# A fixed four-engine order for the prologue of a fused attention and two-MoE kernel, with three weight slices of the first batch ahead of the rest, and two attention units scored a phase earlier

## The chip, the cores and the metric

The kernel runs on one core of one Trainium2 chip. The metric is the device time of one execution in microseconds (us); the time of a kernel is the median of its runs. A profile is one execution taken by the hardware profiler; its span runs from the first to the last instruction. Engines: PE (matmul), PEld (its weight loads), DVE, ACT, POOL, and SP, which issues all the DMAs.

## The reference

```python
def _attn_ref(q, k, v, phi):                  # 4 batches, 8 heads, 576 rows, head_dim 64, 32 memory slots
    a = np.exp(phi - phi.max(axis=2, keepdims=True))
    a = a / (a.sum(axis=2, keepdims=True) + 1e-09)
    k_m = np.einsum('bhsm,bhsd->bhmd', a, k)
    v_m = np.einsum('bhsm,bhsd->bhmd', a, v)
    scores = 1 / np.sqrt(64) * np.matmul(q, k_m.transpose(0, 1, 3, 2))
    attn = np.exp(scores - scores.max(axis=-1, keepdims=True))
    attn = attn / (attn.sum(axis=-1, keepdims=True) + 1e-09)
    return np.matmul(attn, v_m)
# its output as 2304 tokens x 512, then
h = np.maximum(np.maximum(x @ w1, x @ w2), x @ w3);  x = h @ w_out         # 512 -> 768 -> 512
h = x @ w_in;  y = (np.maximum(h, 0) + np.log1p(np.exp(-np.abs(h)))) @ w_out2   # 512 -> 2048 -> 512
```

## The kernel before

**Units.** The attention is cut into eight units: unit u is batch u // 2 and four of its heads. For each unit the code has these steps: `load_phi`, `load_x` (i = 0 is k, i = 1 is v) and `load_q` issue its DMAs; `att_max` and `att_exp` make exp(phi - max); `att_x` multiplies that with k or v (its first call also makes the column sums) and scales the result into `kvd`; `att_tr` turns it into `kT` or into a part of the tile `v`; `att_q` transposes q on PE and ACT copies it into `qT`; `att_sc` makes the scores; `att_sm0`, `att_sm1`, `att_sm2` are the softmax over the 32 slots (transposes and maximum on DVE; subtraction on POOL or DVE, then exp on ACT; sum and reciprocal on DVE, then the multiplication); `att_fin` transposes on DVE into `aT` and splits the result into a high part `ah` (ACT) and a rest `al`.

**First MoE, by pairs of batches.** `pp` 0 is units 0 to 3 (batches 0 and 1), `pp` 1 is units 4 to 7. attn @ v_m is never made. Instead, for each of six slices j of 128 columns of w1, w2 and w3, the slice is multiplied with v_m (`u_mm`, `u_mr`; L545 and L563 to L565) into a tile pair `uh`, `ul`, and `m1(i, bl, c)` multiplies that with `ah` and `al` (L591): 18 matmuls of 128x288, three products for each float32 product; then ACT and DVE take the maximum of the three results (L597 to L599) out of PSUM into `h`. Here i is 0 to 5 for `pp` 0 and 6 to 11 for `pp` 1, bl the batch of the pair (bl 0 reads units 0 and 1, bl 1 units 2 and 3), c the half of its rows. `phase_a` runs what is left of the 24 m1 of a pair, each a numbered slot; `phase_o` runs the 18 slots of `m1out` (L633 to L635), 12 matmuls of 128x384 each. So the program is: prologue, `phase_a(0)`, `phase_o(0)`, `phase_a(1)`, `phase_o(1)`, and then 96 equal blocks of the second MoE (L843, L875).

**Weights.** They come as 64-bit floats, as pairs of int32. `w_load(i, hf)` fetches half a slice with three DMAs into one of two buffers `wraw`; `w_conv` and `Conv.a` make floats of it: an ACT scaling of the upper word (L242), then two DVE operations (L245, L246), the last of which frees the buffer. A slice has four parts p of 128 rows.

**What sets the order.** A scheduler orders the instructions of each engine before the program runs, by its own estimate of when each can start and by the order in which the code writes them. For the prologue that order is the list `PLAN`, a row for each step (`ax` for `att_x`, `ca` for a conversion, and so on). In the phases the tables `C["att"]`, `C["scs"]`, `C["wo"]` give the slot behind which a step is written: `att` the first part of units 4 to 7, all in `phase_a(0)`; `scs` the six steps from `att_q` to `att_fin` of units 4 to 7, all in `phase_o(0)`; `wo` the conversions of w_out. On the chip each engine goes through its list in that order. PSUM gives PE six buffers for u, m1 and m1out (`psm`) and two (`pst`) for the rest from unit 4 on.

Of the kernel before, what the change touches and what calls it, by code (L numbers as in the profile page):

```python
# [20 lines left out]
PLAN = [  # L21
    ('ph', 0),
    ('ph', 1),
    ('wl', 0, 0),
    ('ld', 0, 1),
    ('ld', 1, 1),
    ('ph', 2),
    ('wl', 0, 1),
    ('ld', 0, 0),
    ('ld', 1, 0),  # L30
    ('q', 0),
    ('q', 1),
# [96 lines left out]
    'wo_off': {(4, 0): 1, (5, 3): 0, (5, 1): -1, (3, 3): -1, (3, 0): 0, (4, 1): -2, (3, 2): 0, (5, 0): -1, (3, 1): 1, (5, 2): -2, (4, 3): 0, (4, 2): 0},  # L129
# [6 lines left out]
def fused_kernel(ctx: ExitStack, tc: tile.TileContext, q, k, v, phi, w1, w2, w3, w_out, m_in, m_out, out):  # L136
# [82 lines left out]
    class Conv:  # L219
# [14 lines left out]
        def a(self):  # L234
            raw, n = self.raw, self.n
# [28 lines left out]
    @contextmanager  # L264
    def behind(u):
        with ExitStack() as st:
            for i in INS[u]:
                st.enter_context(tc.issue_after(i))
            yield
# [58 lines left out]
    def att_max(u):  # L328
# [6 lines left out]
        nc.vector.tensor_tensor(out=mx[0:SREM], in0=mx[0:SREM], in1=ph[0:SREM, :, R4], op=ALU.max)  # L335
        st = pst()
        nc.tensor.matmul(st[:, 0:P], mx.rearrange("p h m -> p (h m)"), ident, start=True, stop=True)
        mc = t_p.tile([P, 1], F32, tag="mc", name="mc", bufs=2)
        nc.vector.tensor_reduce(out=mc, in_=st[:, 0:P], op=ALU.max, axis=AX.X)
        md = t_p.tile([P, P], F32, tag="md", name="md", bufs=2)  # L340
        nc.vector.tensor_scalar(out=md, in0=ident, scalar1=mc, scalar2=None, op0=ALU.mult)
        nc.tensor.matmul(st[:, P:2 * P], onesq, md, start=True, stop=True)
        d["ma"] = st[:, P:2 * P].rearrange("p (h m) -> p h m", h=4)

    def att_exp(u):
        d = U[u]
        ph, ma = d.pop("ph"), d.pop("ma")
        nc.vector.tensor_tensor(out=ph, in0=ph, in1=ma.unsqueeze(2).to_broadcast([P, 4, R4 + 1, M]), op=ALU.subtract)
        et = t_p.tile([P, R4 + 1, 4, M], F32, tag="et", name="et", bufs=2)
        nc.scalar.activation(out=et.rearrange("p r h m -> p h r m"), in_=ph, func=AF.Exp)  # L350
        d["et"] = et.rearrange("p r h m -> p r (h m)")

    def att_x(u, i):
# [14 lines left out]
        if new_ri:  # L368
            for r in range(R4 + 1):
                for h in range(4):  # L370
                    a = slice(32 * h, 32 * h + 32)
                    k = slice(0, P if r < R4 else SREM)
                    nc.tensor.matmul(xp[a, D:D + 2], et[k, r, a], ones[k], start=(r == 0), stop=(r == R4))
            ri = t_p.tile([P, 1], F32, tag="ri", name="ri", bufs=2)
            nc.vector.tensor_scalar(out=ri, in0=xp[:, D:D + 1], scalar1=1e-9, scalar2=None, op0=ALU.add)
            nc.vector.reciprocal(out=ri, in_=ri)
            d["ri"] = ri
        kvd = t_p.tile([P, D], F32, tag="kvd", name="kvd", bufs=3)
# [3 lines left out]
    def att_tr(u, i):  # L382
# [5 lines left out]
        for s in range(2):  # L388
            nc.tensor.matmul(st[64 * s:64 * s + 64, P:2 * P], kvd, pick2[:, s], start=True, stop=True)
        sv = st[:, P:2 * P].rearrange("p (a c) -> p a c", a=2)  # L390
# [14 lines left out]

    def att_kv(u):
        att_x(u, 1)
        att_x(u, 0)

    def att_trs(u):  # L410
        att_tr(u, 1)
        att_tr(u, 0)

    def att_q(u, remeng="act"):
# [10 lines left out]
        for s in range(2):  # L425
            qp = ps()
            for r in range(R4):
                nc.tensor.transpose(qp[:, r * P:(r + 1) * P], x[:, s, r], ident)
            cast("act", qT[:, s, 0:R4 * P], qp)
        rem = ps()  # L430
        for s in range(2):
            nc.tensor.transpose(rem[:, s * SREM:(s + 1) * SREM], xr[:, 2 * s:2 * s + 2].rearrange("p h d -> p (h d)"), ident[0:SREM, 0:SREM])
        cast(remeng, qT[:, :, R4 * P:S], rem[:, 0:2 * SREM].rearrange("p (s c) -> p s c", s=2))
        d["qT"] = qT

    def att_sc(u):
# [4 lines left out]
        for c in range(2):  # L441
# [4 lines left out]
            d["sc"].append(sc)  # L446

    def att_sm0(u):
# [8 lines left out]
        d["mx"] = mx  # L457

    def att_sm1(u, sub="pool"):
# [3 lines left out]
        e.tensor_tensor(out=sT, in0=sT, in1=d.pop("mx").to_broadcast([P, NJB, 32]), op=ALU.subtract)  # L463
        nc.scalar.activation(out=sT, in_=sT, func=AF.Exp, scale=SCALE)

    def att_sm2(u, mul="pool"):
# [5 lines left out]
        nc.vector.reciprocal(out=sm, in_=sm)  # L472
        e = nc.vector if mul == "dve" else nc.gpsimd
        e.tensor_tensor(out=sT, in0=sT, in1=sm.to_broadcast([P, NJB, 32]), op=ALU.mult)

    def att_fin(u, lo="dve"):
# [74 lines left out]

    def u_mr(i, p):
# [23 lines left out]
    def m1(i, bl, c):  # L576
        pp, j = i // NJ, jof(i)
# [18 lines left out]
        h = h_t[j][:, o:o + HS]  # L596
        nc.scalar.activation(out=t0, in_=xs[0], func=AF.Copy)  # L597
        nc.vector.tensor_tensor(out=t0, in0=t0, in1=xs[1], op=ALU.max)
# [58 lines left out]
    def phase_a(pp, bg, us):  # L657
# [4 lines left out]
        def add_conv(slot, i, p):  # L662
            o = slot + C["wo_off"].get((i, p), 0)
            bg2[o].append(lambda: conv(i, p))
            if pp:
                bg2[o + 1].append(lambda: CK["w", i, p].b())
# [6 lines left out]
        for j in range(1 if pp == 0 else 0, NJ):  # L673
# [4 lines left out]
            if i == 1:  # L678
                four = [(0, 1, 0), (0, 1, 1), (1, 1, 0), (1, 1, 1)]
            for n, a in enumerate(four):  # L680
                main.append(lambda i=i, a=a, n=n, nxt=nxt: (m1(*a), u2(i + 1, n - us) if nxt and n in (us, us + 1) else None))
            if j + 2 < NJ:
# [18 lines left out]
    def conv(i, p):  # L701
        w_conv(i, p)
        u = 1 if i == 1 else 3 if 2 < i < NJ else None
        if u is None:
            CK["w", i, p].a()
            return
        with behind(u):
            CK["w", i, p].a()

    new_vT(0)  # L710
    STEPS = dict(ph=load_phi, ld=load_x, q=load_q, mx=att_max, ex=att_exp, ax=att_x, tr=att_tr, qT=att_q,
                 sc=att_sc, s0=att_sm0, s1=att_sm1, s2=att_sm2, fin=att_fin, wl=w_load, ca=conv,
                 un=u_new, u=u_mm, m1=m1)
    for st in PLAN:
        f = STEPS[st[0]]
        if isinstance(st[-1], dict):
            f(*st[1:-1], **st[-1])
        else:
            f(*st[1:])
# [9 lines left out]
    bg[3].append(lambda: (new_vT(1), load_u(4)))  # L729
# [7 lines left out]
    def held(f, u):  # L737
        with behind(3):
            f(u)

    wcv = {}
    for j in range(NJ):
        def wo_go(j=j):
            wcv[j] = wo_conv(j)
            with behind(3):
# [4 lines left out]
    phase_a(0, bg, C["us0"])  # L750
    bg = defaultdict(list)
    load_q(4)
    for n in range(4):
        u = 4 + n
        for sl, fn in zip(C["scs"][n], (lambda u=u: att_q(u), lambda u=u: (att_sc(u), load_q(u + 1) if u + 1 < 8 else None),
                                       lambda u=u: att_sm0(u), lambda u=u: att_sm1(u, C["s1"][u - 4]),
# [185 lines left out]
```

## Time and profile before

| | us |
|---|---|
| median of 3 runs | 743.45 (742.6 to 746.43) |
| profiled execution, whole | 743.82 |
| its span | 742.0 |
| PE busy | 705.8 |
| DVE, ACT, POOL busy | 406.4, 299.7, 250.0 |

What the profiled execution has beside its span is 1.82 us. A busy share over the whole span mixes stages with different limits, so the stages are read one by one: the prologue to about 56 us, `phase_a(0)` and what is left of the attention to 147.5, `phase_o(0)` to about 206, the passage into `phase_a(1)` to 236, its rest to 287.5, `phase_o(1)` to 340 and the second MoE to the end. The clock granted to PE has two levels in the records, 1.0 (2.4 GHz) and 0.5 (1.2 GHz); it is not recorded before 31.5 us. Transposes and other float32 matmuls of the attention have two records for each instruction, and a few records of m1 are missing.

### The profile page before, as it was taken

To read this page: it belongs to the slowest core of one execution; us is meant where nothing else is said; L and a number is where in the kernel's file an instruction comes from. 1 tells how busy PE (TensorE), PEld (TensorE's weight loads), DVE (VectorE), ACT (ScalarE), POOL (GpSimd) and SP (SyncE) were. 2 spreads that over 40 slices of the span, in tenths; PEclk is the share of its full clock that TensorE was granted. 3 is DMA by queue.
4 is the path that set the end of the run, shared out by engine and by line. 5 is a ranking of instruction groups with operands and counts; after the bars stand their busy time and mean duration, and the time that the engine had idled before them with its cause. 6 is when DMAs were issued, how large, how long until landed. Compare 5 with 4: busy or idle time off the path is not lost. (4 is left out here: it accounts for less than half of the span.)

```text
span 742.0 us, 12241 instructions
## 1 busy us (share of the span) xinstructions
PE 705.8 (95%) x4680; PEld 621.0 (84%) x4680; DVE 406.4 (55%) x780; ACT 299.7 (40%) x628; POOL 250.0 (34%) x239
## 2 busy tenths in 40 slices
PE   4879999999959999989999999999999999999997
PEld 3548777998848999978998988989888989898896
DVE  4557996425588974682333486333794334433343
ACT  2345555336458753552333453222442223222221
POOL 1112233035348414762222353222642223322221
PEclk9979999999988999999999999999999999999999
DMA  9998693502233200440000032000231000011112
GB/s 246 225 244 217 216 258 100 150 1 76 80 99 128 87 1 29 142 144 27 1 0 1 30 113 86 1 1 0 84 117 28 1 1 1 0 44 43 44 42 86
DMA packets 70490, 59.25 MB, mean 80 GB/s; under 512 B 27936, under 2 KB 65312, under 8 KB 70432
## 3 DMA queue, kind: packets, MB, share of 16 engines
q1 hardware_dynamic: 70432, 58.47, 27.3%
q8 instruction: 37, 0.61, 0.3%
q14 instruction: 21, 0.17, 0.1%
HBM read 53.74 MB, written 4.72 MB: 79 GB/s over the span
## 5 line engine op out<-in xcount | busy, mean ns | idle before, releaser
L217 POOL TENSOR_TENSOR gl<-m,gh 128x384 fp32r<-128x384 f32 x96 | 100.5, 1049 | 255.1 <-ACT gh L209 238.2
L849 DVE TENSOR_SCALAR e<-pst 128x384 int32<-128x384 int32 x96 | 53.1, 554 | 135.9 <-PE pst L843 135.8
L851 ACT ACTIVATE L<-e 128x384 f32<-128x384 f32 x96 | 50.3, 524 | 186.6 <-DVE e L849 186.5
L875 PE MATMUL acc<-oh,gh 128*128 128x512 f32 x288 | 113.7, 395 | 0.4 <-ACT gh L209 0.4
L875 PE MATMUL acc<-ol,gh 128*128 128x512 f32 x288 | 113.4, 394 | 0.0
L843 PE MATMUL pst<-yb,ih 128*128 128x384 f32 x384 | 102.1, 336 | 0.0
L591 PE MATMUL psm<-ah,uh 128*128 128x288 f32 x288 | 89.0, 314 | 9.7 <-ACT ah L485 6.9
L591 PE MATMUL psm<-al,uh 128*128 128x288 f32 x288 | 87.3, 304 | 0.6 <-POOL al L217 0.6
L591 PE MATMUL psm<-ah,ul 128*128 128x288 f32 x288 | 86.4, 302 | 0.0
L853 DVE SCALAR_TENSOR_TENSOR m<-pst,L 128x384 f32<-128x384 f32 x96 | 53.3, 556 | 56.0 <-ACT L L851 56.0
L875 PE MATMUL acc<-oh,gl 128*128 128x512 f32 x288 | 82.7, 394 | 0.0
L209 ACT ACTIVATE gh<-m 128x384 fp32r<-128x384 f32 x96 | 50.0, 523 | 63.1 <-DVE m L853 61.2
L843 PEld LDWEIGHTS pst<-yb,ih 128*128 128x128 f32 x384 | 70.0, 188 | 3.5 <-DVE m L853 0.7
L591 PEld LDWEIGHTS psm<-ah,uh 128*128 128x128 f32 x288 | 55.6, 195 | 17.0 <-ACT ah L485 7.7
L843 PE MATMUL pst<-y0h,ih 128*128 128x384 f32 x192 | 65.4, 341 | 2.6 <-DVE m L853 2.5
L843 PE MATMUL pst<-y0h,il 128*128 128x384 f32 x192 | 65.2, 340 | 0.0
L843 PE MATMUL pst<-y0l,ih 128*128 128x384 f32 x192 | 65.2, 340 | 0.0
L843 PE MATMUL pst<-yb,il 128*128 128x384 f32 x192 | 64.4, 335 | 0.0
L875 PEld LDWEIGHTS acc<-oh,gl 128*128 128x128 f32 x288 | 53.6, 187 | 11.4
L875 PEld LDWEIGHTS acc<-oh,gh 128*128 128x128 f32 x288 | 54.0, 187 | 10.5 <-ACT gh L209 0.9
L875 PEld LDWEIGHTS acc<-ol,gh 128*128 128x128 f32 x288 | 54.0, 187 | 9.0
L591 PEld LDWEIGHTS psm<-al,uh 128*128 128x128 f32 x288 | 56.1, 195 | 1.4 <-POOL al L217 1.0
(146 smaller groups left out, 1327.9 us busy)
## 6 DMA issues: line engine op xcount, KB each, us to landing
wraw<-in_moe_w_dram SPq DMA_DIRECT2D x66, 256.0 KB, 3.9
raw<-in_moe_w_in_dram SPq DMA_DIRECT2D x16, 512.0 KB, 3.7
raw<-in_moe_w_out_dram SPq DMA_DIRECT2D x16, 512.0 KB, 3.6
out_dram<-o SPq DMA_DIRECT2D x18, 256.0 KB, 2.2
kvm<-in_v_dram SPq DMA_DIRECT2D x8, 512.0 KB, 6.3
kvm<-in_k_dram SPq DMA_DIRECT2D x8, 512.0 KB, 7.1
wor<-in_moe_w_out_dram SPq DMA_DIRECT2D x6, 512.0 KB, 4.3
ph<-in_phi_dram SPq DMA_DIRECT2D x8, 256.0 KB, 5.8
```

What stands on the lines that cost most here:

```text
L209: nc.scalar.activation(out=dst, in_=src, func=AF.Copy)
L217: return e.tensor_tensor(out=dst, in0=src, in1=hi, op=ALU.subtract)
L591: nc.tensor.matmul(x, l[:, t, ws], r[:, cs], start=(n == 0), stop=(n == 5))
L843: nc.tensor.matmul(hx, l[:, ds], r[:, cs], start=(n == 0), stop=(n == 3 * ND - 1))
L849: nc.vector.tensor_scalar(out=e.bitcast(I32), in0=hx.bitcast(I32), scalar1=0x7FFFFFFF, scalar2=None, op0=ALU.bitwise_and)
L851: nc.scalar.activation(out=L, in_=e, func=AF.Softplus, scale=-1.0)
L853: nc.vector.scalar_tensor_tensor(out=m, in0=hx, scalar=0.0, in1=L, op0=ALU.max, op1=ALU.add)
L875: nc.tensor.matmul(acc[0][t], l[:, t * P:(t + 1) * P], r, **kw)
```

## The change

`PLAN` becomes a list of single-engine stages: each step is a generator that yields where it goes from one engine to the next, each repetition of a step in the list runs its next stage, and the whole list stands in a `manual_schedule` for PE, DVE, ACT and POOL, which keeps on these four the order in which the stages are written. SP is not among them. In the new list units 0 and 1 go first, with less in between; u(0) is made for bl 0 alone; then m1 of i = 0, 1 and 2 for bl 0; units 2 and 3 are finished among these; then bl 1. Fourteen slots stay for `phase_a(0)` instead of 20, and the tables are written anew for them. `scs` has negative numbers, which are slots of `phase_a(0)`: unit 4 is scored there except for its last step, unit 5 except for its last, unit 6 begins there; unit 7 keeps slots of `phase_o(0)`, but earlier ones.

```diff
 PLAN = [
-    ('ph', 0),
-    ('ph', 1),
-    ('wl', 0, 0),
...
+    ('ph', 0), ('ph', 1), ('ld', 0, 1), ('mx', 0), ('mx', 0), ('mx', 1), ('wl', 0, 0), ('mx', 0), ('mx', 1),
...
+    ('ca', 2, 1), ('m1', 1, 0, 0), ('sc', 3), ('wl', 3, 0), ('ax', 2, 0), ('ca', 2, 1), ('ax', 2, 0),
...
-    'load5': 5,
-    'att': [[9, 9, 10, 11, 11], [10, 12, 12, 13, 13], [13, 13, 15, 15, 15], [15, 18, 19, 21, 21]],
-    'wo': [[4, 5, 5], [6, 7, 7], [11, 11, 14], [11, 13, 17], [21, 22, 24], [23, 23, 23]],
-    'scs': [[4, 4, 4, 4, 5, 6], [5, 5, 5, 6, 6, 7], [6, 6, 6, 7, 10, 10], [8, 11, 12, 13, 14, 18]],
+    'load5': 0,
+    'cv0': {2: (0, 0, 1, 1), 3: (3, 4, 5, 6)},
+    'order': ('PE', 'DVE', 'Activation', 'Pool'),
+    'hold': (2, 3),
+    'att': [[1, 1, 2, 3, 3], [2, 4, 4, 5, 5], [6, 6, 8, 8, 8], [8, 10, 11, 12, 12]],
+    'wo': [[0, 1, 1], [2, 3, 3], [4, 5, 6], [6, 7, 8], [10, 11, 12], [12, 13, 13]],
+    'scs': [[-8, -7, -7, -6, -5, 0], [-6, -4, -4, -3, -2, 1], [-1, 0, 1, 2, 3, 4], [2, 4, 4, 5, 6, 8]],
+    'q4': 3,
...
+    def ca_step(i, hf):
+        cs = []
+        for p in (2 * hf, 2 * hf + 1):
+            cs.append(w_conv(i, p))
+            cs[-1].top()
+        yield
+        for c in cs:
+            c.join()
...
-    for st in PLAN:
-        f = STEPS[st[0]]
...
+    gens, DONE = {}, set()
+    order = {getattr(mybir.EngineType, x) for x in C["order"]}
+    with tc.manual_schedule(engines=order):
+        for st in PLAN:
+            if st[0] in LOADS:
+                LOADS[st[0]](*st[1:])
+                continue
+            if st not in gens:
+                gens[st] = STEPS[st[0]](*st[1:])
+            if next(gens[st], DONE) is DONE:
+                DONE.add(st)
...
-    bg[3].append(lambda: (new_vT(1), load_u(4)))
+    bg[0].append(lambda: (new_vT(1), load_u(4)))
...
+            (bg if sl < 0 else bgo)[sl + 14 if sl < 0 else sl].append(fn)
```

On SP, around the loads of the third weight slice (`wraw` is w1, w2, w3; `kvm`, `kvr` are k and v of a unit, `qn` and `qnr` q of units 0 to 3, `qr` of unit 4, `wor` the first part of w_out). Before:

```order
L183 DMA wraw<-in_moe_w_dram 128x2x256 x6
L183 DMA ph<-in_phi_dram 128x4x128
L183 DMA ph<-in_phi_dram 64x4x32
L183 DMA kvm<-in_v_dram 128x4x256
L183 DMA kvr<-in_v_dram 64x4x64
L183 DMA kvm<-in_k_dram 128x4x256
L183 DMA kvr<-in_k_dram 64x4x64
L183 DMA wor<-in_moe_w_out_dram 128x1024
```

Here the six `wraw` are the second slice; units 4 and 5, `wor` and q of unit 4 follow, and then the third slice, at the head of a row of twelve. The changed kernel, a few rows behind the second slice:

```order
L120 DMA ph<-in_phi_dram 128x4x128
L120 DMA ph<-in_phi_dram 64x4x32
L120 DMA kvm<-in_v_dram 128x4x256
L120 DMA kvr<-in_v_dram 64x4x64
L120 DMA kvm<-in_k_dram 128x4x256
L120 DMA kvr<-in_k_dram 64x4x64
L120 DMA wor<-in_moe_w_out_dram 128x1024
L120 DMA wraw<-in_moe_w_dram 128x2x256 x6
L120 DMA qr<-in_q_dram 128x4x64 x4
```

The first six rows are unit 5; unit 4 stands in the same form just ahead of them. So the third slice (the six `wraw`) still has units 4 and 5 and `wor` ahead of it; only q of unit 4 has gone behind it.

On ACT in the changed kernel, from the second m1 slice on. `wh` and `wl` from `wraw` are the conversion of the third slice, two instructions for each half; `mt` empties PSUM behind an m1, `kvd`, `kT`, `sT` and `v` are steps of units 2 and 3:

```order
L182 ACTIVATE wh<-wraw 128x384
L182 ACTIVATE wl<-wraw 128x384
L605 ACTIVATE mt<-psm 128x288
L182 ACTIVATE wh<-wraw 128x384
L182 ACTIVATE wl<-wraw 128x384
L330 ACTIVATE kvd<-psm,ri 128x64
L605 ACTIVATE mt<-psm 128x288
L345 ACTIVATE kT<-psm 128x128
L146 ACTIVATE hh<-h 128x384
L444 ACTIVATE sT<-sT 128x576
L330 ACTIVATE kvd<-psm,ri 128x64
L350 ACTIVATE v<-psm 128x2x64
```

Before, at its conversion of the third slice, ACT has the softmax of units 2 and 3 nearly behind it:

```order
L485 ACTIVATE ah<-aT 128x576
L464 ACTIVATE sT<-sT 128x576
L209 ACTIVATE hh<-h 128x384
L548 ACTIVATE uh<-psm 128x384 x3
L242 ACTIVATE wh<-wraw 128x384
L242 ACTIVATE wl<-wraw 128x384
L548 ACTIVATE uh<-psm 128x384
L242 ACTIVATE wh<-wraw 128x384
L242 ACTIVATE wl<-wraw 128x384
L597 ACTIVATE mt<-psm 128x288 x2
L485 ACTIVATE ah<-aT 128x576
```

The conversion of the third slice has moved ahead of the scores of units 2 and 3.

On PE at the passage from `phase_o(0)` to `phase_a(1)`, the scores of unit 7 (`pst<-qT,kT`). Before, they stand inside the m1 of the second pair:

```order
L565 MATMUL psm<-wl,vh 128x384
L444 MATMUL pst<-qT,kT 64x288 x2
L563 MATMUL psm<-wh,vh 128x384
L564 MATMUL psm<-wh,vl 128x384
L565 MATMUL psm<-wl,vh 128x384
L444 MATMUL pst<-qT,kT 64x288 x2
L591 MATMUL psm<-ah,uh 128x288 x2
```

In the changed kernel they stand among the matmuls of `m1out`, and some 40 further matmuls of `m1out` follow before the first m1:

```order
L643 MATMUL psm<-hh,wol_1526 128x384
L421 MATMUL pst<-qT,kT 64x288 x2
L644 MATMUL psm<-hlo,woh_1525 128x384
L642 MATMUL psm<-hh,woh_1525 128x384
L643 MATMUL psm<-hh,wol_1526 128x384
L644 MATMUL psm<-hlo,woh_1525 128x384
L642 MATMUL psm<-hh,woh_1525 128x384
L643 MATMUL psm<-hh,wol_1526 128x384
L421 MATMUL pst<-qT,kT 64x288 x2
L644 MATMUL psm<-hlo,woh_1525 128x384
```

Then come two m1 of bl 0 (36 matmuls) and 12 of L567 to L569, and only then the first m1 that reads units 6 and 7.

## Rows read from the trace of the kernel before

**Rows 1.** The profile's page: busy time of each engine, share of the span, instructions

```profile
PE 705.8 (95%) x4680; PEld 621.0 (84%) x4680; DVE 406.4 (55%) x780; ACT 299.7 (40%) x628; POOL 250.0 (34%) x239
```

**Rows 2.** Busy us by stretch (instructions), then granted clock, DMA share, GB/s

```profile
0.00:56.00 56.00, 39.73 (x599) 25.47 (x599) 28.29 (x76) 19.90 (x46) 6.95 (x17) 0.90 0.94 239
...
80.00:147.50 67.50, 67.22 (x762) 54.28 (x759) 50.87 (x130) 34.95 (x89) 18.55 (x23) 1.00 0.61 178
147.50:206.00 58.50, 58.34 (x462) 51.95 (x462) 25.05 (x50) 28.66 (x63) 25.48 (x24) 1.00 0.22 56
206.00:236.00 30.00, 20.96 (x113) 17.64 (x112) 24.98 (x44) 19.94 (x44) 17.30 (x17) 0.77 0.34 106
```

**Rows 3.** PE in order of time, 205 to 226 us [idle before, releaser]

```profile
211.80 0.71 PE L444 MATMUL pst<-qT,kT 128*64 128x288 f32 x4
217.66 0.85 PE L591 MATMUL psm<-ah,uh 128*128 128x288 f32 x2 [5.16 <-ACT ah L485]
...
219.54 0.44 PE L591 MATMUL psm<-ah,ul 128*128 128x288 f32 x1
219.78 0.44 PE L591 MATMUL psm<-al,uh 128*128 128x288 f32 x1
...
222.20 0.85 PE L591 MATMUL psm<-ah,uh 128*128 128x288 f32 x2 [1.74 <-ACT ah L485]
```

**Rows 4.** PE's groups from 206 to 236 us: busy, mean ns, idle before

```profile
L591 PE MATMUL psm<-al,uh 128*128 128x288 f32 x29 | 10.3, 360 | 0.6 <-POOL al L217 0.6
L591 PE MATMUL psm<-ah,ul 128*128 128x288 f32 x29 | 9.9, 346 | 0.0
L591 PE MATMUL psm<-ah,uh 128*128 128x288 f32 x25 | 9.3, 390 | 8.4 <-ACT ah L485 6.9 <-DVE mt L598 1.0 <-DVE ul L574 0.5
```

**Rows 5.** PE in order of time at the full clock, 249 to 256 us

```profile
249.13 0.34 PE L564 MATMUL psm<-wh,vl 128*128 128x384 f32 x1
249.30 0.34 PE L565 MATMUL psm<-wl,vh 128*128 128x384 f32 x1
...
250.00 0.29 PE L591 MATMUL psm<-ah,uh 128*128 128x288 f32 x1
250.13 0.29 PE L591 MATMUL psm<-al,uh 128*128 128x288 f32 x1
```

**Rows 6.** The stretch at the lower clock, columns as in rows 2

```profile
215.90:229.50 13.60, 8.98 (x31) 7.65 (x32) 10.33 (x18) 8.68 (x19) 5.24 (x5) 0.50 0.40 136
```

**Rows 7.** DVE in order of time, the end of unit 7

```profile
222.18 0.76 DVE L217 TENSOR_TENSOR al<-aT,ah 128x576 fp32r<-128x576 f32 x1 [0.75 <-ACT ah L485]
```

**Rows 8.** The loads around the third slice, columns as in rows 2

```profile
60.00:70.00 10.00, 10.00 (x67) 7.04 (x66) 8.62 (x19) 5.83 (x13) 3.01 (x3) 1.00 1.05 255
```

**Rows 9.** The page's DMA issues: KB each, median us to landing

```profile
qr<-in_q_dram SPq DMA_DIRECT2D x16, 128.0 KB, 3.6
```

**Rows 10.** ACT in order of time, the casts of the third slice

```profile
68.91 0.56 ACT L242 ACTIVATE wh<-wraw 128x384 f32<-128x384 f32 x1 [1.05 <-DMA wraw<-in_moe_w_dram]
...
71.07 0.55 ACT L242 ACTIVATE wh<-wraw 128x384 f32<-128x384 f32 x1 [0.79 <-DMA wraw<-in_moe_w_dram]
```

**Rows 11.** PE in order of time: first m1, and the third u (80.00, 80.32)

```profile
55.85 0.61 PE L591 MATMUL psm<-ah,uh 128*128 128x288 f32 x1
...
79.62 0.54 PE L545 MATMUL psm<-wh,v 128*64 128x384 f32 x1
...
80.00 0.49 PE L545 MATMUL psm<-wh,v 128*64 128x384 f32 x1
...
80.32 0.49 PE L545 MATMUL psm<-wh,v 128*64 128x384 f32 x1
```

**Rows 12.** ACT's and DVE's groups from 0 to 100 us, columns as in rows 4

```profile
L246 DVE SCALAR_TENSOR_TENSOR wh<-wraw,wh 128x384 int32<-128x384 int32 x10 | 5.9, 592 | 0.0
...
L245 DVE TENSOR_SCALAR wh<-wh 128x384 int32<-128x384 int32 x11 | 5.0, 455 | 11.7 <-ACT wh L242 11.7
...
L242 ACT ACTIVATE wh<-wraw 128x384 f32<-128x384 f32 x11 | 6.1, 550 | 22.0 <-DMA wraw<-in_moe_w_dram 22.0
```

More of the change, by code (lines that the diff above doesn't have):

```diff
@@ L264, in behind @@
     @contextmanager
-    def behind(u):
+    def behind(us):
         with ExitStack() as st:
-            for i in INS[u]:
-                st.enter_context(tc.issue_after(i))
+            for u in us:
+                for i in INS[u]:
+                    st.enter_context(tc.issue_after(i))
             yield
@@ L424, in att_q, with pe, ev @@
         ps = psm if u < 4 else pst
-        for s in range(2):
+        def pe(s):
             qp = ps()
+            if s == 2:
+                for a in range(2):
+                    nc.tensor.transpose(qp[:, a * SREM:(a + 1) * SREM], xr[:, 2 * a:2 * a + 2].rearrange("p h d -> p (h d)"),
+                                        ident[0:SREM, 0:SREM])
+                return qp
             for r in range(R4):
                 nc.tensor.transpose(qp[:, r * P:(r + 1) * P], x[:, s, r], ident)
[L429 to L433, printed above, removed]
+            return qp
+        def ev(s, qp):
+            if s == 2:
+                cast("act", qT[:, :, R4 * P:S], qp[:, 0:2 * SREM].rearrange("p (s c) -> p s c", s=2))
+            else:
+                cast("act", qT[:, s, 0:R4 * P], qp)
+        if u >= 4:
+            for s in range(3):
+                ev(s, pe(s))
+                yield
+        else:
+            qps = []
+            for s in range(3):
+                qps.append(pe(s))
+                yield
+            for s in range(3):
+                ev(s, qps[s])
+                if s < 2:
+                    yield
         d["qT"] = qT
@@ L550, in u_mm, with u_step @@
             nc.vector.tensor_tensor(out=Uj[i][bl][1][:, t, :], in0=xs[bl], in1=Uj[i][bl][0][:, t, :], op=ALU.subtract)
+    def u_step(i, bl):
+        if i not in Uj:
+            Uj[i] = [None, None]
+        Uj[i][bl] = uh, ul = tuple(a_p.tile([P, 2, 3 * P], F32R, tag=f"u{x}", name=f"u{x}", bufs=3) for x in "hl")
+        xs = []
+        for t in range(2):
+            assert ("v", bl, t) in CK
+            CK["u", i, t, bl] = 1
+            X = psm()[:, 0:3 * P]
+            for e in range(2):
+                p = 2 * t + e
+                assert CK["w", i, p].done
+                nc.tensor.matmul(X[64 * e:64 * e + 64], vT[0][:, p, bl], wj_t[i, p], start=True, stop=True)
+            xs.append(X)
+        yield
+        for t in range(2):
+            nc.scalar.activation(out=uh[:, t, :], in_=xs[t], func=AF.Copy)
+        yield
+        for t in range(2):
+            nc.vector.tensor_tensor(out=ul[:, t, :], in0=xs[t], in1=uh[:, t, :], op=ALU.subtract)
     def u_mr(i, p):
@@ L576, in m1, with m1_step @@
     def m1(i, bl, c):
+        go(m1_step(i, bl, c))
+    def m1_step(i, bl, c):
         pp, j = i // NJ, jof(i)
@@ L655, in run, with phase_a @@
                     f()
-    def phase_a(pp, bg, us):
+    def phase_a(pp, bg, u0):
         i0 = pp * NJ
@@ L671, in u2 @@
             u_mm(i, a)
-        for j in range(1 if pp == 0 else 0, NJ):
+        for j in range(2 if pp == 0 else 0, NJ):
             i = i0 + j
@@ L737, in held @@
     def held(f, u):
-        with behind(3):
-            f(u)
+        with behind(PL):
+            go(f(u))
     wcv = {}
@@ L744, in wo_go @@
             wcv[j] = wo_conv(j)
-            with behind(3):
+            with behind(PL):
                 wcv[j][0].a()
```

178 lines of the change are left out of this document (55 added, 123 removed), and 25 rows, old and new, of the table PLAN.

## The prediction

> **What bounds the kernel now.** I read the page first. PE is busy for 705.8 of 742.0 us and no other engine for more than 55% of the span [rows 1], so the end moves only where PE is idle or slow. A share over the whole span does not tell where, so the stretches come next [rows 2]. From 80 to 206 us and from 236 on, PE is full at clock 1.00: nothing that is merely moved inside these stretches changes the end. It is not full in the prologue (39.73 of 56 us) and at the passage between the pairs (20.96 of 30 us, mean clock 0.77). The diff touches these two places; the order of the second MoE and the weight conversions ahead of it stay, and I count them at nothing.
>
> What waits at the passage is seen in PE's list: the scores of unit 7 are issued at 211.80, the next m1 starts at 217.66 after 5.16 us of waiting for `ah`, and 1.74 us more come at 222.20, for `ah` again [rows 3]. With the smaller waits (for `al` 0.6, DVE `mt` 1.0, `ul` 0.5) that is 9.0 us of idleness [rows 4]. Behind it the clock is 0.50 for 13.6 us, in which PE is busy for 8.98 [rows 6]: m1 matmuls start 0.24 us apart there [rows 3], and 0.13 at the full clock [rows 5]. At the full clock the same work takes half, so the clock costs 4.5 us. The passage loses 13.5 us.
>
> In the prologue the question is when PE has work for good. The first m1 starts at 55.85, and the third u at 79.62, with its next pairs 0.32 us apart [rows 11]; between the two PE is nearly full.
>
> **The passage: what goes.** Units 4 and 5 are scored in `phase_a(0)` and unit 7 some 40 `m1out` matmuls before the end of `phase_o(0)`. From the last scores of unit 7 to its first use lie now 40 x 0.17 = 7 us, two m1 of bl 0 (36 x 0.13 = 4.7 us) and 12 matmuls of 0.17 (2.1 us) [rows 5], together 14 us. The chain they must cover, from those scores to `al`, took from 212.5 (211.80 + 0.71) to 222.9 (222.18 + 0.76), so 10.4 us [rows 3, 7]. It fits, with 3.5 us to spare. So the waits for `ah` and `al` go (7.5 us) and, with no long idleness, the stretch at the lower clock (4.5 us): -12. The 1.5 us for `mt` and `ul` I leave, since DVE is busy for 24.98 of the 30 us there and keeps its conversions [rows 2]. Bounds: -13.5 (nothing waits) and -4 (the spare 3.5 us are eaten and half of it returns).
>
> The Trainium skill, in "TensorE: Matmul & The Clock Gate", "What's actually happening", says that the throttled state is the default and that activity releases it. The trace agrees: 0.50 right behind 5.16 us of idleness [rows 3, 6]. By that rule idleness opened elsewhere is paid in the same way; if the four m1 behind the new waits of the prologue ran at 0.24, that would be 4 x 18 x 0.11 = 7.9 us more, and the kernel would come out at 744.
>
> **The scoring that moves into `phase_a(0)`.** It is the same PE work, taken from one full stretch and put into another: 0. What covers it are DVE's free 16.6 of 67.5 us from 80 to 147.5 [rows 2]; unit 4 brings some 5 us of DVE work, an estimate from the chain of 10.4 us above, of which about half stands on DVE. If that cover is gone, PE waits for the two `pst` buffers, up to +4. I take 0.
>
> **The prologue: what is gained first and lost later.** Each step is the same instruction as before, so PE's work is unchanged; what counts is when PE has done an equal amount. With fewer steps ahead of it, the first m1 comes when units 0 and 1 are through their softmax and q of unit 3, which PE must transpose before it, has landed. phi of unit 2 and k of units 2 and 3 come behind it now, by their shapes 0.29 + 2 x 0.59 MB; at 255 GB/s [rows 8] that is 5.8 us. I put the first m1 at about 41 us instead of 55.85. But four m1 (i = 0 and 1, 72 x 0.13 = 9.4 us) are all that can be done until the third slice is there, and its loads come late: on SP units 4 and 5 and `wor` are still ahead of them. Only q of unit 4 has gone behind, 4 x 128 KB [rows 9] and a 64 KB rest, 0.59 MB or 2.3 us at 255 GB/s. ACT's casts of the two halves waited for their loads until 68.91 and 71.07 [rows 10]; the queue has no slack, its share being 1.05 from 60 to 70 [rows 8]. So the second half lands at about 68.5 now.
>
> Here the fixed order bites. ACT has these casts directly behind the first m1 of i = 1, and behind them the steps of units 2 and 3 and the `mt` that empties PSUM for the next m1. Two casts take 1.1 us, and DVE's four joins 2.1 us [rows 12], partly beside each other: 71. Then the scores of unit 3 go through DVE, and those of unit 2 half a chain later: 71 + 10.4 + 5 = 86 us until unit 2's `al` (10.4 is the chain above, the 5 an estimate from it). PE meanwhile makes three half u (four instructions each, 3 x 4 x 0.32 = 3.8 us, from about 75), the two m1 of i = 2 (4.7 us) and one half u more (1.3 us): 85. So m1(1, 1, 0) starts at about 86 us.
>
> By then six m1 and six half u (24 instructions) are done. Before, at 79.62, six m1 and a third of one (114 matmuls by the printed order) were done and four half u (16 instructions). The changed kernel is two half u ahead (2.6 us) and a third of an m1 behind (0.8 us): before, the same work was done at 81.4. The prologue loses 86 - 81.4 = +4.6. Bounds: if nothing queues behind the casts, PE goes on at 71 with 3.8 + 4.7 + 1.3 us and reaches the point at 81, -0.5; if units 2 and 3 were through by then and the loads 5 us faster, -6; if the m1 behind the waits run at 0.24, +4.6 + 7.9 = +12.5.
>
> The Trainium skill, in "PSUM — Partial Sum Buffer", "Engine vs sequencer instructions", says that the queues of ScalarE, VectorE and GpSimdE are strictly first in, first out. The trace agrees as far as it goes: ACT sat 22.0 us in front of such casts [rows 12]. It speaks against this change; were it otherwise, the prologue would come out at the -0.5 above and the kernel at 731.
>
> **The sum.** 742.0 - 12 + 0 + 4.6 = 734.6 us of span, and 1.8 us beside it: 736.4 for an execution like the profiled one. That one (743.82) lies 0.4 above the median of its runs, so 736.0.
>
> **Rivals.** *The slices come early* (0.20). The third slice or its casts do not hold the rest up, as the early start would have it, and the prologue gains 2 us. For it: DVE and ACT are idle for half the prologue [rows 2]. Against it: the loads' order and their full share. 742 - 2 - 13.5 + 1.4 = 728.
>
> *The passage keeps its price elsewhere* (0.17). Unit 7 has 3.5 us to spare on a DVE that is busy for five sixths there; if its order puts conversions first, PE waits again, clock included, and only 4.5 us are gained. 742 - 4.5 + 4.6 + 1.4 = 743.5. In this way the change would not do what it says, though the scores are issued earlier.
>
> *Slower: ACT's queue behind the third slice* (0.13). One place, the two casts. Each us that the slice lands after 68.5 is a us for everything behind. With the slice 5 us late (a load ahead of it on SP that waits for its buffer) and four m1 at the lower clock the prologue loses 4.6 + 5 + 7.9 = 17.5: 742 + 17.5 - 12 + 1.4 = 749. It is slower from a loss of 16 on. Against it: the buffers of units 4 and 5 are free long before SP comes to them.
>
> **Chances.** The forecast has 0.50, with 731 to 740 of its own. A measurement of this kernel can tell about 0.5% (3.7 us) from no change. Faster: nearly all of the forecast (0.47) and the early slices (0.20), 0.67; same: the third case and the forecast's edge, 0.20; slower 0.13. The range goes from the early case to short of the slower one and leaves out what lies at the bounds of several terms at once: 727 to 746.
>
> **What would show it.** Right: first m1 at 38 to 44 us; ACT idle before a cast of `wraw` at 62 to 69 us, with PE idle for some us at the same time and clock 0.5 in part; from about 88 us PE full; at the passage, no wait for `ah` of more than 1 us and no stretch at 0.5. Wrong in the prologue if PE is full from 50 us on, or if it is not until 95; wrong at the passage if PE waits there for `ah` or `al` as before, or for DVE for more than 4 us in all.

## The result and the profile after

The changed kernel takes 748.37 us (median of 12 runs, 746.84 to 750.45) against 743.3 us for the kernel before beside it (12 runs): ratio 1.0072, 95% interval [1.0054, 1.0091]. It is slower by about 5 us, where 736.0 was forecast. The profiled execution has a span of 745.8 us, 3.8 more than before. Over the whole span PE's busy time is the same [rows 1], so as a sum the loss is idle time:

```profile
PE 705.3 (95%) x4680; PEld 616.8 (83%) x4680; DVE 407.0 (55%) x780; ACT 299.5 (40%) x628; POOL 249.2 (33%) x239
```

To find where it arises I cut both traces where the same m1 work is done: at m1(1, 1, 0), the seventh m1 in both, at the first `m1out`, and at the last m1 of the second pair. For before, the first cut is the 81.4 us of the prediction, 0.33 us into that m1. Busy time by these stretches, columns as in [rows 2]; before:

```profile
0.00:81.40 81.40, 64.12 (x750) 44.97 (x751) 49.57 (x123) 32.88 (x76) 13.76 (x23) 0.92 0.91 232
81.40:149.40 68.00, 67.72 (x768) 55.55 (x767) 49.92 (x129) 35.02 (x90) 17.30 (x21) 1.00 0.59 174
149.40:287.40 138.00, 128.80 (x933) 119.08 (x932) 90.35 (x179) 77.31 (x171) 58.41 (x54) 0.95 0.22 63
287.40:742.00 454.60, 445.13 (x2235) 401.38 (x2233) 216.51 (x351) 154.48 (x293) 160.51 (x141) 1.00 0.13 44
```

and after:

```profile
0.00:84.20 84.20, 61.76 (x757) 42.49 (x757) 48.74 (x119) 33.02 (x76) 12.37 (x22) 0.92 0.87 225
84.20:162.80 78.60, 75.33 (x795) 59.99 (x794) 57.04 (x144) 38.31 (x97) 20.52 (x24) 0.98 0.53 158
162.80:291.40 128.60, 123.13 (x901) 113.11 (x901) 84.23 (x168) 73.74 (x164) 56.12 (x52) 1.00 0.21 63
291.40:745.80 454.40, 445.03 (x2234) 401.20 (x2233) 216.98 (x351) 154.48 (x293) 160.19 (x141) 1.00 0.14 44
```

The prologue loses 2.8 us, the m1 phase 10.6, the passage and its surroundings gain 9.4, and the rest 0.2: +3.8. The first cut is not quite the same work: at 81.4 the kernel before has made five half u (40 records) where the changed one has six (48), and two m1 matmuls more. That is 1.3 - 0.3 = 1.0 us of PE work, so of equal work the prologue loses about 1.8 us and the m1 phase about 11.6.

The m1 phase is the surprise, and there the loss is not idle time alone: PE is idle for 3.3 us (before 0.3) and busy for 75.3 (before 67.7). PE in order of time behind 89.9 us, and the granted clock right behind that:

```profile
89.90 0.29 PE L598 MATMUL psm<-ah,ul 128*128 128x288 f32 x1
92.83 0.37 PE L598 MATMUL psm<-ah,uh 128*128 128x288 f32 x1 [2.64 <-DVE ul L554]
```

```profile
93.30:96.70 3.40, 3.40 (x17) 3.40 (x16) 2.87 (x10) 0.41 (x1) 0.00 (x0) 0.50 0.95 265
```

PE waits 2.64 us for the last `ul` of the prologue (u of i = 0 for bl 1), and then starts 15 matmuls 0.24 instead of 0.13 us apart, from 93.30 to 96.64: 1.5 us more. DVE in that time, in which it has no gap:

```profile
83.81 0.75 DVE L154 TENSOR_TENSOR al<-aT,ah 128x576 fp32r<-128x576 f32 x1
84.47 0.42 DVE L278 TENSOR_TENSOR m<-ph 128x256 f32<-128x256 f32 x1
...
86.42 0.42 DVE L190 SCALAR_TENSOR_TENSOR cg<-wor,cg 128x256 int32<-128x256 int32 x1
86.75 0.28 DVE L280 TENSOR_TENSOR mx<-mx,ph 64x128 f32<-64x128 f32 x1
...
88.39 1.43 DVE L189 TENSOR_SCALAR wl<-wl 128x384 int32<-128x384 int32 x2
89.73 0.82 DVE L279 TENSOR_TENSOR mx<-m 128x128 f32<-128x128 f32 x1
90.47 1.07 DVE L190 SCALAR_TENSOR_TENSOR wh<-wraw,wh 128x384 int32<-128x384 int32 x1
91.47 0.28 DVE L286 TENSOR_REDUCE mc<-pst 128x1 f32<-128x128 f32 x1
...
92.14 1.01 DVE L554 TENSOR_TENSOR ul<-psm,uh 128x384 fp32r<-128x384 f32 x2
```

ACT had its `uh` ready by 85.4, but between unit 2's `al` and this `ul` DVE goes through phi maxima of units 4 and 5, half-slices of w_out and joins of later slices (a join is the two DVE operations of a conversion, L189 and L190), with one emptying of m1 (`mt` and `h`, 0.9 us) among them. But for that one, none is needed soon. Some of the joins stand in the fixed list; the others, the maxima and w_out could go ahead because they are held behind units 2 and 3 only, and the last `ul` of the list stands behind those.

At the passage the waits for `ah` and the stretch at 0.50 [rows 3, 6] are gone. What PE and ACT show there instead:

```profile
220.89 0.34 PE L569 MATMUL psm<-wl,vh 128*128 128x384 f32 x1
223.89 0.41 PE L567 MATMUL psm<-wh,vh 128*128 128x384 f32 x1 [2.66 <-DVE ul L578]
...
232.10 0.37 PE L598 MATMUL psm<-ah,uh 128*128 128x288 f32 x1 [1.09 <-DVE ul L578]
```

```profile
216.21 5.08 ACT L146 ACTIVATE y0h<-ya 128x384 fp32r<-128x384 f32 x12
221.19 0.51 ACT L146 ACTIVATE wh<-cg 128x384 fp32r<-128x384 f32 x1
221.61 0.96 ACT L574 ACTIVATE uh<-psm 64x384 fp32r<-64x384 f32 x2
```

`ul` is only the last link. The twelve casts `y0h`, which only the second MoE reads, stand in one row ahead of the `uh` that PE's next u needs.

The casts of the third slice, for [rows 10], and PE's wait behind them:

```profile
63.30 0.54 ACT L182 ACTIVATE wh<-wraw 128x384 f32<-128x384 f32 x1 [8.48 <-DMA wraw<-in_moe_w_dram]
...
65.63 0.56 ACT L182 ACTIVATE wh<-wraw 128x384 f32<-128x384 f32 x1 [1.05 <-DMA wraw<-in_moe_w_dram]
```

```profile
64.64 0.61 PE L598 MATMUL psm<-ah,uh 128*128 128x288 f32 x1 [4.99 <-ACT mt L605]
```

### The profile page after: what moved, and what is told of

The parts are those of the page before. It is cut to its first block, busy times and chain, and to the rows that moved or that the text cites. A ratio compares the mean times of both kernels' runs of the same rounds, so it can differ in the third digit from the quotient of the medians.

```text
span 745.8 us, 12231 instructions
## 1 busy us (share of the span) xinstructions
PE 705.3 (95%) x4680; PEld 616.8 (83%) x4680; DVE 407.0 (55%) x780; ACT 299.5 (40%) x628; POOL 249.2 (33%) x239
## 5 line engine op out<-in xcount | busy, mean ns | idle before, releaser
L598 PE MATMUL psm<-ah,uh 128*128 128x288 f32 x288 | 90.9, 316 | 10.8 <-ACT mt L605 6.2
```

The costliest lines, as they stand in the source:

```text
L598: nc.tensor.matmul(x, l[:, t, ws], r[:, cs], start=(n == 0), stop=(n == 5))
```

## The experiments

Times are medians of 4 to 12 runs; the kernel before had 742.55, 743.32, 743.23 and 743.5 us beside e1 to e4, e5 to e8, e9 to e12, and e13 and e14.

**e1 and e4: the two halves of the change, each alone.** e1 gives the changed kernel the old table of the score steps, e4 gives the kernel before the new one. Both also move the load of q of unit 4, e4 those of the later units too.

```diff
 e1 (changed kernel)
...
-    'scs': [[-8, -7, -7, -6, -5, 0], [-6, -4, -4, -3, -2, 1], ...
+    'scs': [[4, 4, 4, 4, 5, 6], [5, 5, 5, 6, 6, 7], ...
...
-    bg[C["q4"]].append(lambda: load_q(4))
+    bgo[0].append(lambda: load_q(4))
 e4 (kernel before)
...
-    'scs': [[4, 4, 4, 4, 5, 6], [5, 5, 5, 6, 6, 7], ...
+    'scs': [[-8, -7, -7, -6, -5, 0], [-6, -4, -4, -3, -2, 1], ...
...
+            (bg if sl < 0 else bgo)[sl + 20 if sl < 0 else sl].append(fn)
```

> The changed kernel with one part undone: the table of the score steps is that of before again, so all four units are scored in the m1out phase. My theory (the two losses lie in DVE's list at 84 to 93 us and in ACT's list at the passage, the scoring itself costs the m1 phase only its own PE time, about 3 us): the m1 phase gets about 3 us shorter and keeps its wait of about 2.6 us for ul at 90 us; the passage waits for ah again and runs at 0.5 for a stretch; 748.4 + 6.8 = about 755. Rival (scoring units 4 and 5 beside the m1 is what slowed the m1 phase): the wait at 90 us goes too, the m1 phase gets 8 to 10 us shorter, and the time stays at 747 to 750.

> The kernel before with one part of the change alone: the table of the score steps is the new one, its negative slots counted from the end of a 20-slot m1 phase, and q of unit 4 is loaded earlier. The prologue is that of before. My theory (the scores' new places give back the waits for ah and the clock at the passage, and cost nothing elsewhere): no wait for ah of more than 1 us and no half-clock stretch at the passage, 743.4 - 8 = about 735.5. Rival (scoring beside the m1 slows that phase): the passage gains as much, but the m1 phase grows by 4 to 6 us more than the moved 3, 739 to 743.

e1: 752.1 us, ratio 1.0128 [1.011, 1.0145]. e4: 736.32 us, 0.9912 [0.9897, 0.9927]. The m1 phase and the passage in e4, to be laid beside the second and third row of before above:

```profile
81.40:152.10 70.70, 70.44 (x677) 56.31 (x676) 52.91 (x134) 38.05 (x94) 18.73 (x23) 1.00 0.59 177
152.10:281.90 129.80, 125.66 (x1027) 116.93 (x1026) 88.76 (x176) 73.25 (x167) 56.70 (x53) 0.99 0.21 63
```

The early scores make the m1 phase 2.7 us longer and give back 8.2 later. About 3.3 us of their own matmuls go in, the k and v products of one unit, about 2 us, go out behind the first `m1out`, and the rest is spread. A short half-clock stretch stays in e4 (mean clock 0.99), which I had not expected. In e1 PE waits 5.22 us for `ah` at the passage again, and the m1 phase still has its wait:

```profile
94.43 0.37 PE L598 MATMUL psm<-ah,uh 128*128 128x288 f32 x1 [2.65 <-DVE ul L554]
...
230.90 0.85 PE L598 MATMUL psm<-ah,uh 128*128 128x288 f32 x2 [5.22 <-ACT ah L467]
```

```profile
85.40:159.30 73.90, 69.80 (x772) 56.31 (x771) 53.00 (x136) 35.90 (x92) 17.35 (x22) 1.00 0.53 161
```

The wait for `ul` is there without the early scores. The m1 phase, which begins at 85.65 here, takes 73.7 us instead of 78.6: of the 4.9 less, about 3 are the scores' own matmuls, and 1.5 the stretch at 0.50, which this trace does not have although the wait is as long. So the early scores did not cause the rest of that phase's loss. e1 came out 3 us below my number, between theory and rival. Each half alone: the scores -6.2, the new prologue +9.6. In the changed kernel the scores are worth 748.4 - 752.1 = -3.7, so the two do not simply add.

**e3: DVE's later work behind the last `ul`.** `hold` names what the later work (conversions, phi maxima, w_out) is issued behind on its engine.

```diff
-    'hold': (2, 3),
+    'hold': (2, 3, ('ul', 0, 1)),
...
-            nc.vector.tensor_tensor(out=ul[:, t, :], in0=xs[t], in1=uh[:, t, :], op=ALU.subtract)
+            last = nc.vector.tensor_tensor(out=ul[:, t, :], in0=xs[t], in1=uh[:, t, :], op=ALU.subtract)
+        INS["ul", i, bl] = (last.ins,)
```

> The changed kernel with one edit: what is queued on DVE behind units 2 and 3 (conversions of the fourth slice on, first halves of w_out, phi maxima of units 4 and 5) is queued behind the last ul of the prologue as well. My theory (PE's wait of 2.64 us at 90 us and the half clock of 3.4 us behind it come from the DVE work that went ahead of that ul): no wait of more than 0.5 us from 85 to 100 us, no 0.5 clock at 93 us, 748.4 - 4.2 = about 744. Rival (DVE has too much to do from 80 to 96 us in any order, and the loads behind its conversions come later still): a wait of 2 to 4 us comes again between 90 and 115 us, 747 to 750.

739.51 us, 0.9964 [0.9949, 0.9979]: 8.9 below the changed kernel, twice what I expected. DVE and the m1 phase:

```profile
86.20 0.75 DVE L154 TENSOR_TENSOR al<-aT,ah 128x576 fp32r<-128x576 f32 x1
...
90.64 1.01 DVE L554 TENSOR_TENSOR ul<-psm,uh 128x384 fp32r<-128x384 f32 x2
```

```profile
85.80:156.90 71.10, 69.75 (x790) 56.41 (x791) 55.38 (x143) 37.25 (x98) 20.86 (x24) 1.00 0.60 177
```

`ul` comes 4.4 us behind `al` instead of 8.3, PE does not wait, the clock is 1.00. The phase from m1(1, 1, 0) (about 86.6 here) is 70.3 us instead of 78.6; about 67.0 of before, by equal work, and the 2.7 of the scores make 69.7. So DVE's row cost some 8 us, of which wait and clock show 2.64 + 1.5; where the other 4 sat, no single wait of the trace shows. The span of this execution is only 5.1 us shorter. It is the slowest of e3's twelve (742.53 us): ahead of the edited part its third slice came 2.4 us later (ACT's first cast of it at 65.69 instead of 63.30), and the passage took 0.6 us more.

**e2: the `y0h` casts behind the `uh` of slices 7 to 10.**

```diff
+        INS["u", i] = (last.ins,)
...
-        cast("act", y0[dm][0][:, cs], y[:, cs])
+        with behind((("u", 7 + dm),)):
+            cast("act", y0[dm][0][:, cs], y[:, cs])
```

> The changed kernel with one edit: the twelve ACT casts y0h that stand ahead of the uh of the second pair's second slice are queued behind it, three each behind the uh of slices 7, 8, 9 and 10. My theory (these 5.1 us of casts in one row make PE wait 2.66 us for ul at the passage): that wait falls below 0.5 us, no new wait of more than 1 us between 210 and 260 us, 748.4 - 2.7 = about 745.5. Rival (DVE's conversions hold ul at the passage anyway, or the casts now hold mt): the wait stays or moves, 747.5 to 749.

745.75 us, 1.0042 [1.0022, 1.0063], 2.6 less. The interval overlaps that of the changed kernel, [1.0054, 1.0091]; the same edit is worth 3.4 and 3.0 below (e5 against e3, e7 against e6). The wait of 2.66 is gone. The longest left at the passage is the first of these two. The second, further on, is new: behind 232.10 the changed kernel has no wait above 0.35 us up to the last m1.

```profile
223.43 0.40 PE L599 MATMUL psm<-ah,uh 128*128 128x288 f32 x1 [0.98 <-ACT mt L606]
...
242.40 0.38 PE L599 MATMUL psm<-ah,uh 128*128 128x288 f32 x1 [1.15 <-DVE ul L579]
```

**e6 and e9: the third slice ahead of units 4 and 5 and w_out on SP**, with e3's edit (e6) and alone (e9).

```diff
+            INS["wl", i, hf] = (nc.sync.dma_start(...).ins,)
...
     def load_u(u):
-        load_phi(u)
-        load_x(u, 1)
-        load_x(u, 0)
+        with behind((("wl", 2, 1),)):
+            load_phi(u)
+            load_x(u, 1)
+            load_x(u, 0)
...
-        dma(out=wr, in_=w_out[j * P:(j + 1) * P])
+        with behind((("wl", 2, 1),)):
+            dma(out=wr, in_=w_out[j * P:(j + 1) * P])
```

> The kernel of e3 with one more edit: the loads of units 4 and 5 and of w_out are queued on SP behind the last load of the third weight slice. My theory (what the new prologue still loses against the one of before, about 3.5 us, is PE's wait for the third slice, which stands behind about 3.5 MB of other loads): ACT's casts of the third slice run at 55 to 60 us instead of about 66, PE's idle time around 65 us goes, m1 of the second pair of rows starts about 4 us earlier, 739.5 - 4 = about 735.5. Rival (the chain of units 2 and 3 through DVE and ACT binds, not the slice): the casts come earlier and the time stays at 738.5 to 740.5.

> The changed kernel with the load edit of e6 alone: units 4, 5 and w_out behind the third slice on SP; DVE's list and ACT's casts as in the changed kernel. My theory (the three causes are separate and add): casts of the third slice at about 57 us, m1 of the second pair of rows 4 us earlier, PE's wait for the last ul stays at 2 to 4 us; 748.4 - 4.5 = about 744. Rival (the slice earlier only lengthens PE's wait behind DVE's row): the wait for ul grows to 6 us or more, 747 to 749.

e6: 734.34 us, 0.9884 [0.9859, 0.9909]; e9: 741.49, 0.9976 [0.9956, 0.9995]. In e6 the casts no longer wait for a load, and PE is not idle for them:

```profile
57.19 0.54 ACT L182 ACTIVATE wh<-wraw 128x384 f32<-128x384 f32 x1
57.63 0.54 ACT L182 ACTIVATE wl<-wraw 128x384 f32<-128x384 f32 x1
...
58.36 0.56 ACT L182 ACTIVATE wh<-wraw 128x384 f32<-128x384 f32 x1
```

Alone the loads are worth 6.9 us, with e3 5.2: the two causes share a little. The stretches of e9 up to m1(1, 1, 0) and up to the first `m1out`:

```profile
0.00:77.80 77.80, 59.89 (x756) 41.55 (x756) 49.24 (x119) 33.26 (x77) 12.31 (x22) 0.93 0.93 244
77.80:154.30 76.50, 74.95 (x795) 59.94 (x794) 55.47 (x144) 38.13 (x97) 21.99 (x24) 0.98 0.55 161
```

The prologue is 6.4 us shorter than in the changed kernel. The m1 phase is 2.1 us shorter, with a wait for `ul` of 1.54 us. (This execution is 2.4 us faster than e9's median.)

**e5, e7, e8, e12: combinations.** e5 is e2 with e3, e7 all three edits, e8 is e4 with e2's edit, e12 is e1 with all three.

> The changed kernel with both edits of e2 and e3: DVE's later work behind the last ul of the prologue, and the y0h casts behind the uh of slices 7 to 10. In the trace of e3 the passage still has waits of 3.2, 1.2 and 0.6 us for ul and mt. My theory (two separate queues, so the gains add): these waits fall to under 1.5 us in all, 739.5 - 2.6 to 3.5 = about 736.5. Rival (e3 removed the slack that e2's edit used): 739 to 740.

> The changed kernel with all three edits (DVE's later work behind the last ul, the y0h casts later, the third slice's loads ahead of units 4, 5 and w_out). My theory: the gains add, 748.4 - 8.9 - 2.8 - 4 = about 732.5. Rival (the prologue's chain of units 2 and 3 binds): as e5, 736 to 737.

> The kernel of e4 (before, with the new table of the score steps alone) with the y0h casts behind the uh of slices 7 to 10. In e4 PE waits at the passage for 0.5, 0.7, 0.8 and 1.5 us, and eight of the twelve casts stand in front of an mt there. My theory: a gain of 1 to 2 us, about 735. Rival (the casts fill idle time of ACT there): 736 to 737.

> The kernel of e1 (new prologue, score steps in the m1out phase as before) with the three edits of e7. It shows what the new prologue is worth by itself once its queues are mended. My theory (prologue and scores add): 731.3 + 6 = about 737.5, against 752.1 in e1 and about 743 before. Rival (the mended queues need the early scores): 743 or more.

Measured: e5 736.15 (0.9903 [0.9874, 0.9932]), e7 731.33 (0.9838 [0.9811, 0.9865]), e8 735.16 (0.9892 [0.9867, 0.9918]), e12 738.32 (0.9939 [0.9915, 0.9964]). All lie within 1.2 us of the theory's numbers; the gain of e8 over e4, 1.2 us, is within their intervals. The new prologue alone goes from +9.6 to -4.9 us once three rows are ordered otherwise.

**e11 and e14: further along the same queue.** e11 is e7 with the second slice loaded ahead of k of units 2 and 3 and phi of unit 2. e14 also moves the fourth slice's conversion back in the list.

```diff
 e11
-                LOADS[st[0]](*st[1:])
+                late = st in (('ld', 2, 0), ('ld', 3, 0), ('ph', 2))
+                with behind((('wl', 1, 1),) if late else ()):
+                    LOADS[st[0]](*st[1:])
 e14
-    ('ca', 3, 0), ('u', 2, 1), ('s2', 2), ('ca', 3, 1), ('ca', 3, 0), ('m1', 2, 0, 1), ('m1', 2, 0, 0),
+    ('u', 2, 1), ('s2', 2), ('m1', 2, 0, 1), ('m1', 2, 0, 0),
...
+    ('m1', 1, 1, 0), ('u', 0, 1), ('u', 0, 1), ('m1', 1, 1, 0), ('ca', 3, 0), ('m1', 1, 1, 1), ('m1', 1, 1, 0),
...
```

> The kernel of e7 with k of units 2 and 3 and phi of unit 2 queued on SP behind the second weight slice. In e7 PE is idle from 44.5 to 48.5 us for that slice. My theory: 2.5 to 3 us less of idleness there, and unit 2 is not needed so early; 731.3 - 2.5 = about 729. Rival (k of units 2 and 3 then come too late for the m1 of their batch): 731 to 734.

> The kernel of e11 with the conversion of the fourth slice moved in the list from ahead of the last m1 of i = 2 to behind the first m1 of the second rows. In e11 PE is idle from 72.3 to 77.1 us for an mt that stands on ACT behind a cast which waits for that slice's load. My theory (the same mechanism as in the forecast's slower rival, one slice later): that wait goes, 726.9 - 3 = about 724. Rival (the later joins free the buffers later, and the fourth and fifth slices are missed in the m1 phase): 727 or more.

e11: 726.89 us, 0.9784 [0.9767, 0.9802]. ACT and PE show what is left:

```profile
75.79 0.55 ACT L182 ACTIVATE wh<-wraw 128x384 f32<-128x384 f32 x1 [3.82 <-DMA wraw<-in_moe_w_dram]
76.24 0.53 ACT L182 ACTIVATE wl<-wraw 128x384 f32<-128x384 f32 x1
76.67 0.39 ACT L607 ACTIVATE mt<-psm 128x288 f32<-128x288 f32 x1
```

```profile
77.12 0.83 PE L547 MATMUL psm<-wh,v 128*64 128x384 f32 x1 [4.85 <-ACT mt L607]
```

e14: 725.09 us, 0.9762 [0.973, 0.9793]. That wait is gone, and this has the lowest median, 18 us below before. The step from e11, 1.8 us, is smaller than the 3 us expected, and the two intervals overlap.

**e10 and e13: without the fixed order**, in the changed kernel (e10) and in e11 (e13).

```diff
-    with tc.manual_schedule(engines=order):
+    with ExitStack():
```

> The changed kernel without the fixed order: the same list of stages, but the scheduler orders the four engines in the prologue as it does elsewhere. My theory (what cost the time is what stands ahead of the third slice on SP, ahead of the last ul on DVE and ahead of uh on ACT, not the fixing of an order): in the printed order the twelve y0h no longer stand ahead of uh, the third slice still stands behind units 4 and 5; 744 to 747. Rival of the forecast (the fixed order itself makes the engines queue behind the casts of the third slice): 748.4 - 5 or more, 740 to 743.

> The kernel of e11 (all edits, loads of both early slices ahead) without the fixed order on the four engines. e10 gained 5.7 us by that alone. My theory (e10 gained because its loads and lists came out otherwise, which e11 has already mended by hand): no gain, 727 to 731. Rival (the fixed order as such costs 5 us or more): 721 to 723.

e10: 742.71 us, 0.9985 [0.9968, 1.0001], 5.7 below the changed kernel: inside the rival's range, and my 744 to 747 was missed. In its trace the third slice is still behind units 4 and 5, but on ACT its casts come behind more steps of units 2 and 3 and wait for no load, and PE waits for DVE's joins instead of an `mt`:

```profile
66.92 0.56 ACT L182 ACTIVATE wh<-wraw 128x384 f32<-128x384 f32 x1
```

```profile
70.45 0.86 PE L547 MATMUL psm<-wh,v 128*64 128x384 f32 x2 [2.76 <-DVE wh L190]
```

So in the changed kernel the rival's mechanism, engines queueing behind the casts in a fixed order, was at work; how much of the 5.7 it is, the trace does not show. e13: 732.1 us, 0.9852 [0.9822, 0.9881], 5.2 above e11. The fixed order costs time in the one and saves as much in the other: it has no price of its own here, it fixes whatever it is given.

## Why the prediction was wrong

*The early start.* Right in its mechanism: first m1 at 39.5 us (forecast 41), PE idle for 4.99 us for `mt` behind the third slice's casts, m1(1, 1, 0) at 84.2 (forecast 86). The second half of the slice was cast from 65.6 us on, where 68.5 was forecast for its landing; from one execution to another this moves (68.1 in e3's). The prologue lost 2.8 us to the cut of the forecast, 4.6 was forecast. That cut was about 1 us early: the trace has 108 m1 matmuls ahead of 79.62, six m1 and not a third of one more, and all 864 m1 records of the kernel are in it.

*"PE full from about 88 us" failed.* I took from [rows 2] that nothing merely moved inside a full stretch changes the end. That holds for PE's work and not for the lists of the engines that feed it. I priced the m1 phase at 0, with up to +4 for `pst`; it measured +10.6. For the moved scoring itself that was right in kind: in e4 the phase grows by 2.7 us, and the passage gives them back. But the new prologue leaves one u for the end, and DVE's row ahead of its `ul` cost some 8 us (e3). I worked out the prologue as finished at 86 us and did not read DVE's list from there to the next use. The bound of +12.5 put four m1 at the lower clock behind the waits. The trace has about two: the m1 behind the 4.99 us (18 matmuls 0.24 apart from 64.64 on) and the 15 matmuls behind 93.30.

The rule of strict queues that the prediction weighed for ACT (the Trainium skill, "PSUM — Partial Sum Buffer", "Engine vs sequencer instructions") decided on DVE: the trace agrees, with a `ul` whose input was ready at 85.4 and that began at 92.14.

*The passage: -12 was too much.* The step "the waits for `ah` and `al` go and the lower clock with them" was right. But I left only 1.5 us for `mt` and `ul`; the waits for `ul` were 2.66 and 1.09 us, the larger behind the twelve casts (e2: 2.6 us of time). The moved matmuls taken out, the passage gained 9.4 - 2.7 = 6.7 us, and e4 gains 8.2 - 2.7 = 5.5. The row of casts stood in the changed kernel's order on ACT; I had read there only PE's list.

*A reading without consequence.* PE is not full "from 236 us on": from 287.5 to 340 it is busy for 48.6 of 52.5 us before, at a mean clock of 0.97. The change left that as it was (+0.2 us behind the last m1).

*The sum.* Forecast -12 + 0 + 4.6 = -7.4 of span; measured 2.8 + 10.6 - 9.4 - 0.2 = +3.8. The term that decided against the forecast is the 0, which became 10.6. The slower rival named ACT's queue behind the third slice, with a slice 5 us late and a prologue loss of 17.5. That its 749 lies near the measured 748.4 is luck: the prologue lost 2.8. Its mechanism, an `mt` behind a cast that waits for a load, does cost time: moving the loads alone brings the kernel to 741.5 (e9), as moving DVE's row alone brings it to 739.5 (e3). Both are below before, so neither alone decided the sign. The first was in the forecast's +4.6, the second nowhere.

*Open.* Which waits carry the 4 us of e3 that the trace does not show as idle time, and what in e10's order makes up its 5.7 us.

## What to carry to other kernels

When a unit of work is moved up, read on each engine that feeds PE what now stands between the last input and its use: what is ready early and needed late (casts for a later phase, joins, maxima) fills any gap and must be tied behind the urgent instruction, not behind the one that happened to be last before. Price a reordering to the first use behind it that depends on each engine's row, not to the last step of the moved part. And when a fixed order loses, look first at its ties (what is issued behind what) and at its loads: two ties and the order of the transfers made the same list 21.5 us faster (e11).

## What the runs showed of the hardware

POOL in the changed kernel while PE waited at 90 us, and the second of the two L189 of DVE's row:

```profile
88.55 1.05 POOL L154 TENSOR_TENSOR hlo<-h,hh 128x384 fp32r<-128x384 f32 x1 [7.92 <-ACT hh L146]
89.56 1.57 POOL L154 TENSOR_TENSOR wol<-cg,woh 128x256 fp32r<-128x256 f32 x2
```

```profile
88.66 1.16 DVE L189 TENSOR_SCALAR wl<-wl 128x384 int32<-128x384 int32 x1
```

In just this time (88.55 to 91.13) three of DVE's operations took two to three times as long: 1.16 for this L189 (0.35 for the one before it, which began at 88.39), 0.82 for L279 (0.29 at 94.53 in e3), 1.07 for L190 (0.54 to 0.56 elsewhere). e9 has the same row of DVE beside the same POOL instruction, and there POOL was the slow one:

```profile
81.84 2.16 POOL L154 TENSOR_TENSOR hlo<-h,hh 128x384 fp32r<-128x384 f32 x1 [7.83 <-ACT hh L146]
```

```profile
81.86 0.62 DVE L189 TENSOR_SCALAR wl<-wl 128x384 int32<-128x384 int32 x2
82.39 0.28 DVE L279 TENSOR_TENSOR mx<-m 128x128 f32<-128x128 f32 x1
82.60 0.55 DVE L190 SCALAR_TENSOR_TENSOR wh<-wraw,wh 128x384 int32<-128x384 int32 x1
```

From the start of the first L189 to the start of the last L190 ahead of `ul` the row took 3.3 us in the changed kernel and 1.4 in e9, where only that last L190 was slow (1.15). So POOL's work beside the row is a likely part of PE's 2.64 us. It is not shown: no run changes POOL alone, and spans on POOL are rough. The Trainium skill, in "SBUF — State Buffer", "SBUF: two separate sides", says that VectorE and GpSimd share a port pair, and that of a GpSimd operation and a VectorE operation in a two-port mode or with two SBUF inputs the one that starts first holds it for its whole instruction. The traces agree as far as these rows go: in each, one of the two engines is held up. e3's two `ul`, which read one input from PSUM, kept their 0.5 us each beside POOL.

The clock fell to 0.50 behind PE's 2.64 us of idleness at 90 us, and stayed at 1.00 behind 2.66 us at 221 us (the stretch from 162.8 to 291.4 has a mean of 1.00). It stayed at 1.00 in e1 too, behind the same wait at the same place of the program (2.65 us at 94 us). Idleness of one length is not paid in one way.
